# Squares of the weights behind the fourth hh eviction, and urgent evictions of hh, hl and ysb, in a two-layer mixture-of-experts kernel

## The chip, the cores and the metric

The kernel runs on one core of a Trainium2 chip. The metric is the device time of one execution in microseconds (us), the median of the runs given. One further execution was recorded by the hardware profiler; all rows and times by line below are from it. TensorE is PE in the rows (PEld its weight loads), VectorE is DVE, ScalarE is ACT, GpSimd is POOL, SyncE is SP; a "q" behind an engine's name is its instruction queue.

## The reference

Linear attention with a norm makes `x` of 4608 rows of 512; a first layer of experts sends each row to two of eight experts, a second sends rows with a positive score to one of eight. An expert is two matrices, 512 x 1024 and 1024 x 512, with a ReLU between:

```python
for e in range(E):                                   # first layer, k = 0, 1
    h = np.maximum(x[mask] @ w1[e], 0.0)
    out[mask] += top2_w[mask, k, None] * (h @ w2[e])
...
for e in range(E):                                   # second layer
    h = np.maximum(xc[mask] @ w1[e], 0.0)
    y[mask] = gate_w[mask, None] * (h @ w2[e])
```

## The kernel before

The stages follow each other: attention and routing up to about 240 us, the first layer of experts up to about 1130 us, then the second layer. All is computed in 16-bit pairs (high and low half), so each weight matrix is scaled and split before use.

The first layer runs through 38 groups, n = 0 to 37, of two tiles of 128 rows (three of them of one tile; the last group of an expert may have fewer rows than 256). For each group TensorE does layer 1 in four pieces of 24 matmuls (L227; a one-tile group has two pieces of 48), each into one of the three buffers of the PSUM pool pA. After each piece ScalarE writes `hh`, the ReLU's high half (L235), and VectorE `hl`, the low half (L236), which frees the buffer. Layer 2 (L263) takes for each tile g 16 matmuls with `hh`, in the order of the pieces, and 8 with `hl`; ScalarE scales its result into `ysb` (L1089), SP writes `ysb` to `ydram`, VectorE adds the other expert's row to make `x` (L1093), and GpSimd scatters it. Between the two tiles of layer 2 stand small matmuls that gate the group before (L952, from `x2T`, a DMA transpose of `xh`, which ScalarE and VectorE split out of `x` after a sum of squares `jk`), and behind them matmuls that rank its rows (L995, from `rm`, which VectorE makes of the gate's result).

Beside this runs the preparation of weights. The table `MATS` gives each group at most one matrix: F, a half of the next expert's weights of the first layer, or P, a half of the second layer's (`presplit`, written to DRAM by SP as `wsd`). A matrix takes these steps: a load of 2 MB into `stage` (two buffers) by SP; four squares with a running sum, `wjunk` (L169), on ScalarE; their sum `wsum` (L172) on VectorE; a small matmul over the partitions (L175) on TensorE; the scale `wscl`; four splits, each a copy on ScalarE (L185) and a difference on VectorE (L186), after which the `stage` buffer is free. The load and the squares are written in the matrix's own group (squares at points 4 to 7, after layer 2's first tile), the matmul and the splits in the group after it, at points 0 to 4.

TensorE's order is the order in which the code is written, in all groups. For the other engines it is so only up to group 2 and from group 35 on; between, a scheduler orders each engine's queue by priority, which is the order of the code, and by its own idea of when an instruction's inputs are there. Each queue is then run in that order on the chip: an instruction at the head that waits for a semaphore holds back what stands behind it.

Of the kernel before, what the change touches and what calls it, by code (L numbers as in the profile page):

```python
# [12 lines left out]
AF = mybir.ActivationFunctionType  # L13
# [5 lines left out]
N, D, E, F = 4608, 512, 8, 1024  # L19
# [28 lines left out]
ROUTE = (9, 12, 14, 14, 16, 22, 22, 22, 22, 22, 22, 28, 29, 32, 37, 40, 41, 43, 45, 46, 47, 50, 57, 57, 57, 61, 61)  # L48

LATER = 3  # L50
QTE = "AAVAAVAVVVAVAVVAVAVVVAVAAVAVVVAAAAAAAAAAAAAAVVAAAAAAAAAA"
OSBE = "VVVVAVAAAAAVVAAVAAVAVAAAAAVAAAAAAAAAAAAAAVAAAAAAAAAVAAAA"
SQE = "GGGAAAAAAAAGAAGAAAAAAAAAAAAAAAAAAAAAAAAAAAAAAAAAAAAAAAAA"
# [29 lines left out]
def moe_kernel(ctx: ExitStack, tc: tile.TileContext, q, k, v, g_norm, w_gate, w_noise, noise,  # L83
               w1, w2, w2_skip, w2_gate, w21, w22, out, dbg=None):
    nc = tc.nc
    V, A, G, PE, SP = nc.vector, nc.scalar, nc.gpsimd, nc.tensor, nc.sync
# [3 lines left out]
    wpools = [ctx.enter_context(tc.tile_pool(name="wpool0", bufs=1))]  # L90
    turn = {}
    stg = [None]

    def wtile(shape, dt, name, pool=None):

# [64 lines left out]
    def split_matrix(load, hi, lo, scale, kk, sc, inv):  # L160

        st = stg[0].tile([P, 4096], F32, name="stage")
        load(st)
        acc = tiny.tile([P, 4], F32, name="wacc")
        junk = tiny.tile([P, F], BF16, name="wjunk", bufs=1)
        kw = {} if scale is None else {"scale": scale}
        yield
        for c in range(4):
            A.activation(junk, st[:, F * c:F * c + F], AF.Square, accum_out=acc[:, c:c + 1], **kw)  # L169
            if c == 3:  # L170
                sums = tiny.tile([P, 1], F32, name="wsum")
                V.tensor_reduce(sums, acc, axis=AX.X, op=ALU.add)  # L172
            yield
        ps = pSm[0].tile([P, 1], F32, name="small")
        PE.matmul(ps, ones32, sums, start=True, stop=True)  # L175
        a0, i0 = pow2_scale(ps, kk, "wsc")
        if scale is None:
            V.tensor_copy(sc, a0)  # L178
        else:
            V.tensor_mul(sc, a0, scale)  # L180
        V.tensor_copy(inv, i0)
        for c in range(4):
            yield
            d = slice(F * c, F * c + F)
            A.activation(hi[:, d], st[:, d], AF.Copy, scale=sc)  # L185
            V.scalar_tensor_tensor(lo[:, d], st[:, d], sc, hi[:, d], op0=ALU.mult, op1=ALU.subtract)  # L186
# [44 lines left out]
    def layer1_out(ps, nt, hh, hl, fp):  # L231

        nf = 4 if nt <= P else 2
        fsl = slice(fp * nf, fp * nf + nf)
        A.activation(hh[:, fsl, 0:nt], ps, AF.Relu)  # L235
        V.scalar_tensor_tensor(hl[:, fsl, 0:nt], ps, 0.0, hh[:, fsl, 0:nt], op0=ALU.max, op1=ALU.subtract)  # L236

    def layer1_piece(W, xT, nt, hh, hl, fp):
        layer1_out(layer1_matmuls(W, xT, nt, fp), nt, hh, hl, fp)

    def layer1(W, xT, nt, point=None):
        hh = p2.tile([P, 8, 2 * P], F16, name="hh")
# [40 lines left out]
    with ExitStack() as st:  # L283
# [505 lines left out]
        for b in range(B):  # L789
# [3 lines left out]
            g = gate_columns(b)  # L793
# [252 lines left out]
    def moe1_group(n, W, xg, xT, step, point):  # L1046
        e, i0, ng, nt = groups[n]
        t0 = e * T1 + i0
        aux = xg[:, 0:ng, 512:528]
        gate = tiny.tile([P, 2], F32, name="gate")  # L1050
        if e:
            junk = tiny.tile([P, 8], F32, name="gjunk", bufs=1)
            for g in range(ng):
                V.scalar_tensor_tensor(junk, aux[:, g, 0:8], W[4], at_pos[:, e], op0=ALU.mult, op1=ALU.mult,
                                       accum_out=gate[:, g:g + 1])
        else:
            V.tensor_scalar(gate, aux[:, :, 0], W[4], None, op0=ALU.mult)
        h = layer1(W, xT, nt, point)
        if e:
            val = tiny.tile([P, ng], F32, name="val")  # L1060
            for g in range(ng):
                V.scalar_tensor_tensor(junk, pair_sum[:, e], aux[:, g, 8:9], before, op0=ALU.is_equal, op1=ALU.mult,
                                       accum_out=val[:, g:g + 1])
            fl = tiny.tile([P, ng], F32, name="fl")
            V.tensor_scalar(fl, val, float(TOP - BASE[e]), None, op0=ALU.is_gt)
            nf = tiny.tile([P, ng], F32, name="nf")
            V.tensor_scalar(nf, fl, -BIG, BIG, op0=ALU.mult, op1=ALU.add)
            row = tiny.tile([P, ng], F32, name="orow")
            V.tensor_sub(row, aux[:, :, 9], val)
            V.tensor_sub(row, row, own[:, i0:i0 + ng])  # L1070
            gi = tiny.tile([P, ng], I32, name="gi")
            V.tensor_add(gi, row, nf)
            oi = tiny.tile([P, ng], I32, name="oi")
            V.scalar_tensor_tensor(oi, idxp[:, t0:t0 + ng], -1.0, nf, op0=ALU.add, op1=ALU.add)
            yos = []
            for g in range(ng):
                yo = yob[turn_y[0] % 4]
                turn_y[0] += 1
                G.indirect_dma_start(out=yo, out_offset=None, in_=ydram[0:BASE[e], :],  # L1079
                                     in_offset=bass.IndirectOffsetOnAxis(ap=gi[:, g:g + 1], axis=0),  # L1080
                                     bounds_check=BASE[e] - 1, oob_is_err=False)
                yos.append(yo)
        step(0)
        x2 = p1.tile([P, 2, D], F32, name="x2", bufs=2)[:, 0:ng]
        for g in range(2):
            if g < ng:
                ps = layer2(W, h, g)
                ysb = p2.tile([P, D], F32, name="ysb", bufs=3)
                A.activation(ysb, ps, AF.Copy, scale=gate[:, g:g + 1])  # L1089
                if e < E - 1:  # L1090
                    SP.dma_start(ydram[BASE[e] + (i0 + g) * P:BASE[e] + (i0 + g + 1) * P, :], ysb)
                if e:
                    V.tensor_add(x2[:, g], ysb, yos[g])  # L1093
                    if n >= CUT + 2:
                        G.memset(spacer, 0.0)
                    s = G.indirect_dma_start(out=out, out_offset=bass.IndirectOffsetOnAxis(ap=oi[:, g:g + 1], axis=0),  # L1096
                                             in_=x2[:, g], in_offset=None, bounds_check=N - 1, oob_is_err=False)
                    nodep(s.ins, osc + rd2, "rows of other tokens")
                    osc.append(s.ins)
            step(1 + g)  # L1100
            point(4 + 2 * g)
            point(5 + 2 * g)
        return finalize(e, i0, ng, x2, fl) if e else None
# [188 lines left out]
    for n, (e, i0, _, _) in enumerate(groups):  # L1292
        if n == BEGIN:
            begin.close()
        if n + 1 < len(groups) and n <= BEGIN:
            xs[n + 1] = gather1(*groups[n + 1])
        if n + 2 < len(groups) and n >= BEGIN:
            xs[n + 2] = gather1(*groups[n + 2])
        if n == CUT + 2:
            order.enter_context(tc.manual_schedule(engines=engines))  # L1300
        old, cur = cur, matrix(mats[n])
        if cur:
            next(cur)

        def point(p, old=old, cur=cur):
            if old and p <= 4:
                next(old, None)
                if p == 4:
                    next(old, None)
            if cur and p >= 4:  # L1310
                next(cur)

        def step(k, prev=fin, last=last):
            g = last if k == 0 else prev
            if g is not None:
                next(g, None)
            if k == 0 and n == CUT + 2:
                pick_early()
            for i in range(2):
                for what in AHEAD[i].get((n, k), ""):  # L1320
                    if what == "g":
                        Ra.append(Rows(ahead[i]))
                        for _ in range(2):
                            Ra[i].gather(osc[early_out:])
                    elif what == "s":
                        Ra[i].split()
                    else:
                        dyn_weights(ewi[:, i:i + 1], 2 * i, Wa[i], "ab".index(what))

        step(-1)  # L1330
        if n == CUT + 2:
            splits.close()
            wpools.append(only1.enter_context(tc.tile_pool(name="wpool2", bufs=1)))
            p3 = only1.enter_context(tc.tile_pool(name="p3", bufs=2))
            p4 = xrow_pool.enter_context(tc.tile_pool(name="p4", bufs=1))
            for i in range(4):
                xo.append(p4.tile([P, 1, D], F32, name=f"x2r{i}"))
                G.memset(xo[i], 0.0)
        last = fin
        fin = moe1_group(n, Ws[e], *xs.pop(n), step, point)  # L1340

    next(fin)
# [16 lines left out]
    nr, nt = len(RTILES), 4 + sum(RTILES)  # L1359
# [157 lines left out]
    with flag(0):  # L1517
# [5 lines left out]
        st, cur = 1, 0  # L1523
        while st < nf:
            V.tensor_add(inc[:, 1 - cur, st:nf], inc[:, cur, st:nf], inc[:, cur, 0:nf - st])
            V.tensor_copy(inc[:, 1 - cur, 0:st], inc[:, cur, 0:st])
            cur, st = 1 - cur, st * 2
# [48 lines left out]
        with flag(NX // 2):  # L1576
# [18 lines left out]
            for e in range(E):  # L1595
                W = []
# [22 lines left out]
            for e in range(E):  # L1619
                W = []  # L1620
# [41 lines left out]
```

## Time and profile before

| | |
|---|---|
| time, three runs | 1353.91 us median (1352.23 to 1360.18) |
| profiled execution, its own time | 1369.16 us |
| its span | 1367.1 us |
| mean granted clock of TensorE | 0.957 |
| TensorE, VectorE, ScalarE, GpSimd busy | 1211.8, 818.6, 658.5, 379.0 us |
| moved by DMA | 293.34 MB, 215 GB/s |

The time is the span and about 2 us around it. A clock of 1 is 2.4 GHz; TensorE is granted either that or half of it. Busy time of TensorE is the union of its matmuls; the idle time between them is what the list of waits distributes over those who ended it.

### The profile page before, as it was taken

Reading aid. Unit: us, or ns where it says so; the run is one execution under the profiler, and the core shown is the slowest. Engines: PE = TensorE matmul, PEld = TensorE weight load, DVE = VectorE, ACT = ScalarE, POOL = GpSimd, SP = SyncE. Lnnn points to the kernel's source line nnn. Section 1 sums busy time; section 2 is a strip of 40 time slices with the busy share of each in tenths; the row PEclk is TensorE's granted clock in tenths of the full one; section 3 lists DMA queues with packets and bytes.
Section 4 is the critical chain, followed back from the end, with each engine's and each line's share of the span. In section 5 each row is a group of like instructions: output and inputs, shape, how many; then the busy total and the mean of one; then the engine's idle time right before and its main releaser. Section 6 shows DMA issues by size and latency. Waiting matters only on the chain.

```text
span 1367.1 us, 25295 instructions
## 1 busy us (share of the span) xinstructions
PE 1211.8 (89%) x9341; PEld 855.2 (63%) x9341; DVE 818.6 (60%) x3034; ACT 658.5 (48%) x1209; POOL 379.0 (28%) x454
## 2 busy tenths in 40 slices
PE   6777789997999989998999888798899989999995
PEld 6677677665666656656666655555566657566664
DVE  1667877344776685767568756655777755433321
ACT  1669562355755564656365556444566232222210
POOL 3322342113223223332322232223212322232220
PEclk9978799999999999999999999999999999999998
DMA  9989964867886885976778796869897475586680
GB/s 240 293 240 299 293 163 110 219 197 231 210 268 142 252 220 178 248 235 208 181 245 246 235 289 196 247 111 295 242 253 196 146 197 170 185 236 185 197 270 16
DMA packets 311410, 293.34 MB, mean 215 GB/s; under 512 B 205022, under 2 KB 256222, under 8 KB 307180
## 3 DMA queue, kind: packets, MB, share of 16 engines
q1 hardware_dynamic: 288316, 208.22, 57.5%
q0 software_dynamic: 22384, 82.36, 17.7%
q8 instruction: 75, 1.23, 0.4%
q10 hardware_dynamic: 576, 1.05, 0.2%
q14 instruction: 59, 0.48, 0.1%
HBM read 172.86 MB, written 93.42 MB: 195 GB/s over the span
## 4 chain that ended last, share of the span: by engine, by line
PE 33%; DVE 17%; issue 16%; DMA 16%; ACT 12%; POOL 4%; SPq 1%; POOLq 0%; ACTq 0%; DVEq 0%
PE b L263 16%; DMA stage<-in_moe_w_dram 13%; PE a L227 12%; ACT wjunk L169 4%; DVE wb L186 2%; DVE wa L186 2%; DVE hl L236 2%; ACT presplit L185 1%; PE b L473 1%; PE kvps L408 1%; ACT ysb L1089 1%; ACT hh L235 1%; POOL out_dram L1175 1%; DVE xh L925 1%; DVE rsc L971 1%
## 5 line engine op out<-in xcount | busy, mean ns | idle before, releaser
L227 PEld LDWEIGHTS <-wa 128*128 128x128 f16 x5184 | 465.6, 100 | 79.3 <-issue 14.6
L227 PE MATMUL a<-xT,wa 128*128 128x256 f16 (+6 forms) x3648 | 399.3, 271 | 25.3 <-DVE hl L236 21.8
L263 PE MATMUL b<-wb,hh 128*128 128x512 f16 x1488 | 348.5, 384 | 40.2 <-ACT hh L235 40.0
L263 PEld LDWEIGHTS <-hh 128*128 128x128 f16 x1488 | 140.2, 98 | 208.9 <-ACT hh L235 57.3
L235 ACT ACTIVATE hh<-a 128x512 f16<-128x512 f32 (+5 forms) x186 | 106.7, 577 | 208.4 <-PE a L227 195.2
L236 DVE SCALAR_TENSOR_TENSOR hl<-a,hh 128x512 f16<-128x512 f32 (+5 forms) x186 | 124.7, 674 | 101.5 <-ACT hh L235 90.9
L263 PE MATMUL b<-wb,hl 128*128 128x512 f16 x744 | 178.5, 383 | 0.0
L1096 POOL DMA_INDIRECT out_dram<-x,oi x67 | 69.2, 1032 | 281.0 <-DVE nact L1008 94.6
L1041 POOL DMA_INDIRECT xg<-xrows,idxp x67 | 68.2, 1018 | 274.1 <-DMA xT<-xg 108.5
L263 PEld LDWEIGHTS <-hl 128*128 128x128 f16 x744 | 73.8, 99 | 91.3 <-issue 5.8
L169 ACT ACTIVATE wjunk<-stage 128x1024 bf16<-128x1024 f32 x96 | 101.0, 1052 | 56.7 <-DMA stage<-in_moe_w_dram 50.6
L1089 ACT ACTIVATE ysb<-b,gate 128x512 f32<-128x512 f32 x73 | 49.8, 682 | 155.1 <-PE b L263 129.6
L227 PE MATMUL a<-x2Tr,wa 128*128 128x256 f16 (+1 forms) x1152 | 107.4, 255 | 1.5 <-DMA x2Tr<-xh 1.5
L1079 POOL DMA_INDIRECT yo<-ydram,gi x67 | 74.2, 1107 | 59.9 <-issue 22.7
L186 DVE SCALAR_TENSOR_TENSOR presplit<-stage,wscl,presplit 128x1024 f16<-128x1024 f32 x64 | 80.1, 1280 | 10.6 <-ACT presplit L185 10.1
L185 ACT ACTIVATE presplit<-stage,wscl 128x1024 f16<-128x1024 f32 x64 | 70.5, 1138 | 12.5 <-DVE wscl L178 12.5
L473 PE MATMUL b<-kvbd,qTs 128*128 128x160 f32 x256 | 53.3, 349 | 21.8 <-issue 10.0
L1093 DVE TENSOR_TENSOR x<-ysb,yo 128x512 f32<-128x512 f32 x67 | 46.1, 687 | 40.8 <-ACT ysb L1089 40.7
L921 ACT ACTIVATE jk<-x 128x512 bf16<-128x512 f32 x67 | 42.0, 627 | 50.3 <-DVE x L1093 49.5
L517 POOL TENSOR_TENSOR osb<-osb,rinv 128x1024 f32<-128x1024 f32 (+1 forms) x20 | 37.1, 1854 | 87.0 <-DVE rinv L145 71.4
L473 PEld LDWEIGHTS b<-kvbd,qTs 128*128 128x128 f32 x256 | 43.0, 220 | 26.5 <-issue 10.8
L924 ACT ACTIVATE xh<-x,x2ss 128x512 f16<-128x512 f32 x67 | 44.8, 714 | 26.9 <-DVE x2ss L136 22.8
(356 smaller groups left out, 1566.6 us busy)
## 6 DMA issues: line engine op xcount, KB each, us to landing
stage<-in_moe_w_dram SPq DMA_DIRECT2D x32, 2048.0 KB
wsd<-presplit SPq DMA_DIRECT2D x8, 2056.0 KB
ydram<-ysb SPq DMA_DIRECT2D x64, 256.0 KB
wsd<-presplit SPq DMA_DIRECT2D x8, 2048.0 KB
out_dram<-zeros SPq DMA_DIRECT2D x9, 1024.0 KB
km<-in_k_dram SPq DMA_DIRECT2D x16, 512.0 KB
vm<-in_v_dram SPq DMA_DIRECT2D x16, 512.0 KB
qm<-in_q_dram SPq DMA_DIRECT2D x16, 512.0 KB
```

The costliest lines, as they stand in the source:

```text
L169: A.activation(junk, st[:, F * c:F * c + F], AF.Square, accum_out=acc[:, c:c + 1], **kw)
L185: A.activation(hi[:, d], st[:, d], AF.Copy, scale=sc)
L186: V.scalar_tensor_tensor(lo[:, d], st[:, d], sc, hi[:, d], op0=ALU.mult, op1=ALU.subtract)
L227: PE.matmul(ps[:, i, :], a[:, c, fs], xT[:, b + c, 0:nt], start=(n == 0), stop=(n == 11))
L235: A.activation(hh[:, fsl, 0:nt], ps, AF.Relu)
L236: V.scalar_tensor_tensor(hl[:, fsl, 0:nt], ps, 0.0, hh[:, fsl, 0:nt], op0=ALU.max, op1=ALU.subtract)
L263: PE.matmul(ps, a[:, f, gsl], b[:, f, :], start=(fs.start == 0 and i == 0), stop=(fs.stop == 8 and a is hl and f == 7))
L473: PE.matmul(po[:, i, :], qT[:, i, :], kvb[b % 4][:, h0 + i, :], start=True, stop=True)
L1041: G.indirect_dma_start(out=xg[:, g], out_offset=None, in_=xrows, in_offset=bass.IndirectOffsetOnAxis(ap=idx[:, t0 + g:t0 + g + 1], axis=0))
L1079: G.indirect_dma_start(out=yo, out_offset=None, in_=ydram[0:BASE[e], :], in_offset=bass.IndirectOffsetOnAxis(ap=gi[:, g:g + 1], axis=0), b ...
L1089: A.activation(ysb, ps, AF.Copy, scale=gate[:, g:g + 1])
L1096: s = G.indirect_dma_start(out=out, out_offset=bass.IndirectOffsetOnAxis(ap=oi[:, g:g + 1], axis=0), in_=x2[:, g], in_offset=None, bounds_ ...
```

## The change

Two things, both in the order of the queues. First, from group 3 to group 35 each square of the weights gets an ordering edge, without a semaphore, behind the `hh` that was written last before it in the code; the squares are written after layer 1 of their group, so that is its fourth `hh`. Second, the priority of `hh`, `hl` and of the first layer's `ysb` is raised by 500, so that the scheduler puts them ahead of other instructions of the same engine that it finds ready at the same time. No computation, transfer or buffer is changed.

```diff
+URGENT = 500
...
+    behind = [None, False]
...
         for c in range(4):
-            A.activation(junk, st[:, F * c:F * c + F], AF.Square, accum_out=acc[:, c:c + 1], **kw)
+            with tc.issue_after(behind[0]) if behind[1] else ExitStack():
+                A.activation(junk, st[:, F * c:F * c + F], AF.Square, accum_out=acc[:, c:c + 1], **kw)
...
-        A.activation(hh[:, fsl, 0:nt], ps, AF.Relu)
+        behind[0] = A.activation(hh[:, fsl, 0:nt], ps, AF.Relu).ins
...
-        layer1_out(layer1_matmuls(W, xT, nt, fp), nt, hh, hl, fp)
+        ps = layer1_matmuls(W, xT, nt, fp)
+        with tc.high_priority(offset=URGENT):
+            layer1_out(ps, nt, hh, hl, fp)
...
-                A.activation(ysb, ps, AF.Copy, scale=gate[:, g:g + 1])
+                with tc.high_priority(offset=URGENT):
+                    A.activation(ysb, ps, AF.Copy, scale=gate[:, g:g + 1])
...
         if n == BEGIN:
             begin.close()
+            behind[1] = True
...
         if n == CUT + 2:
             splits.close()
+            behind[1] = False
```

TensorE's queue is the same in both kernels, instruction for instruction. On SP and GpSimd a handful of neighbours change places; in both kernels the load into `stage` stands on SP behind the group's first `ydram` write where the group splits a P half, and ahead of it elsewhere. The changes are on ScalarE and VectorE.

ScalarE at the end of group 16 and the start of group 17, before (line numbers are those of each kernel; x2 means two in a row; the `hh` with 192 columns is the first of group 17):

```order
L185 ACTIVATE wb<-stage,wscl 128x1024
L169 ACTIVATE wjunk,wacc<-stage 128x1024
L235 ACTIVATE hh<-a 128x512
L169 ACTIVATE wjunk,wacc<-stage 128x1024 x3
L1089 ACTIVATE ysb<-b,gate 128x512
L921 ACTIVATE jk,ss_8015<-x_7862 128x512
L973 ACTIVATE rdf<-rdf 128x16
L169 ACTIVATE wjunk,wacc<-stage,gcol 128x1024 x2
L1089 ACTIVATE ysb<-b,gate 128x512
L169 ACTIVATE wjunk,wacc<-stage,gcol 128x1024
L921 ACTIVATE jk,ss_8015<-x_7862 128x512
L235 ACTIVATE hh<-a 128x2x192
```

The same place on ScalarE in the changed kernel, from the fourth split of group 16 to the first `ysb` of group 17:

```order
L188 ACTIVATE wb<-stage,wscl 128x1024
L238 ACTIVATE hh<-a 128x512
L1095 ACTIVATE ysb<-b,gate 128x512
L926 ACTIVATE jk,ss_8015<-x_7862 128x512
L978 ACTIVATE rdf<-rdf 128x16
L1095 ACTIVATE ysb<-b,gate 128x512
L926 ACTIVATE jk,ss_8015<-x_7862 128x512
L238 ACTIVATE hh<-a 128x2x192
L929 ACTIVATE xh<-x_7862,x2ss 128x512 x2
L238 ACTIVATE hh<-a 128x2x192 x3
L172 ACTIVATE wjunk,wacc<-stage 128x1024 x4
L1095 ACTIVATE ysb<-b,gate 128x512
```

The squares of two matrices that stood around the fourth `hh` of group 16, its two `ysb` and the first `hh` of group 17 are gone from there; those of the first of the two are now one block behind group 17's fourth `hh`, and those of the second (with `gcol`) one group later, in the same place.

VectorE in group 17, before:

```order
L236 SCALAR_TENSOR_TENSOR hl<-a,hh 128x2x192
L971 TENSOR_SCALAR rsc_8233<-x2ss,rsk 128x2
L172 TENSOR_REDUCE wsum<-wacc 128x1
L925 SCALAR_TENSOR_TENSOR xh<-x_7862,x2ss,xh 128x512 x2
L236 SCALAR_TENSOR_TENSOR hl<-a,hh 128x2x192 x3
L957 TENSOR_REDUCE rL<-small 128x18
L960 SCALAR_TENSOR_TENSOR act<-rL,fl 128x2
```

VectorE there in the changed kernel:

```order
L976 TENSOR_SCALAR rsc_8233<-x2ss,rsk 128x2
L930 SCALAR_TENSOR_TENSOR xh<-x_7862,x2ss,xh 128x512 x2
L239 SCALAR_TENSOR_TENSOR hl<-a,hh 128x2x192 x3
L175 TENSOR_REDUCE wsum<-wacc 128x1
L962 TENSOR_REDUCE rL<-small 128x18
L965 SCALAR_TENSOR_TENSOR act<-rL,fl 128x2
```

`wsum` has moved with its squares, from ahead of `xh` to behind the last `hl`; behind it stand `rL` and the rest of the gate's small operations, with `x` among them, and `rm`.

## Rows read from the trace of the kernel before

**Rows 1.** The page's first part: busy us (share of the span) xinstructions, by engine

```profile
PE 1211.8 (89%) x9341; PEld 855.2 (63%) x9341; DVE 818.6 (60%) x3034; ACT 658.5 (48%) x1209; POOL 379.0 (28%) x454
```

**Rows 2.** TensorE's waits, 336.8 to 1066.4 us: us in total, times, longest

```profile
PE b L263 <- ACT hh L235: 32.7, 27, 4.3
PE a L227 <- DVE hl L236: 21.8, 9, 4.2
PE small L995 <- DVE rm L988: 5.9, 2, 3.2
PE small L952 <- DMA x2T<-xh: 3.4, 2, 2.3
```

**Rows 3.** Stretches: us, busy by engine (PE first), clock, DMA share, GB/s

```profile
336.80:1066.40 729.60, 664.37 (x5101) 447.46 (x5100) 494.39 (x2010) 412.14 (x707) 207.38 (x211) 0.97 0.81 226
427.30:448.90 21.60, 21.60 (x172) 14.84 (x171) 16.17 (x68) 10.57 (x17) 11.35 (x11) 1.00 0.83 199
...
635.30:661.50 26.20, 21.97 (x170) 15.14 (x169) 11.83 (x58) 10.40 (x21) 4.95 (x5) 0.87 0.59 140
...
804.30:832.30 28.00, 23.80 (x172) 15.00 (x171) 15.95 (x68) 14.94 (x25) 9.95 (x9) 0.94 0.91 262
```

**Rows 4.** Timeline of ScalarE at 638 us: start, duration, instruction, [idle before, releaser]

```profile
638.67 1.15 ACT L169 ACTIVATE wjunk<-stage,gcol 128x1024 bf16<-128x1024 f32 x1 [5.19 <-DMA stage<-in_moe_w_dram]
...
643.41 0.47 ACT L235 ACTIVATE hh<-a 128x384 f16<-128x384 f32 x1
```

**Rows 5.** Timeline of TensorE beside it, layer 1 of group 17

```profile
635.31 6.10 PE L227 MATMUL a<-xT,wa 128*128 128x192 f16 x72
645.64 4.00 PE L227 MATMUL a<-xT,wa 128*128 128x192 f16 x24 [4.23 <-DVE hl L236]
```

**Rows 6.** Timeline of all engines in group 9 (448.9 to 471.3 us)

```profile
461.41 1.05 ACT L169 ACTIVATE wjunk<-stage 128x1024 bf16<-128x1024 f32 x1
...
462.45 0.59 ACT L235 ACTIVATE hh<-a 128x512 f16<-128x512 f32 x1
...
463.09 1.04 PE L263 MATMUL b<-wb,hh 128*128 128x512 f16 x4 [0.69 <-ACT hh L235]
...
463.56 0.40 SPq L200 DMA_DIRECT2D stage<-in_moe_w_dram  x1
...
466.34 0.67 ACT L1089 ACTIVATE ysb<-b,gate 128x512 f32<-128x512 f32 x1
...
468.95 0.17 DVE L988 TENSOR_TENSOR rm<-roh,act 128x16 f16<-128x16 f32 x1
...
471.27 0.17 PE L995 MATMUL small<-rm,tri 128*128 128x16 f16 x1
```

**Rows 7.** The squares (L169), 336.8 to 1066.4 us: duration min/median/max, and waits before them

```profile
L169 ACT ACTIVATE wjunk<-stage x84: 1040/1052/1057, 348.0 to 1037.5; 128x1024 bf16<-128x1024 f32 x84
L169 ACT ACTIVATION_READ_ACCUMULATOR wjunk<-stage x84: 185/188/199, 348.9 to 1038.5; 128x1 f32 x84
L169 ACT ACTIVATE wjunk<-stage,gcol x20: 1134/1147/1149, 406.8 to 892.4; 128x1024 bf16<-128x1024 f32 x20
...
  DMA stage<-in_moe_w_dram: 69.8, 16
```

**Rows 8.** Timeline of all engines in group 8, as layer 2 begins

```profile
438.06 3.62 PE L263 MATMUL b<-wb,hh 128*128 128x512 f16 x16
...
439.09 0.59 ACT L235 ACTIVATE hh<-a 128x512 f16<-128x512 f32 x1
```

**Rows 9.** The chain that ended last, 790 to 960 us: start, us, what

```profile
797.81 0.32 SPq L1091
...
798.18 17.34 DMA stage<-in_moe_w_dram
...
920.93 18.29 DMA stage<-in_moe_w_dram
```

**Rows 10.** The stretch after the stall of group 17; columns as in rows 3

```profile
644.80:651.60 6.80, 5.96 (x31) 4.49 (x31) 3.88 (x13) 2.79 (x7) 0.00 (x0) 0.50 0.51 98
```

## The prediction

> **What bounds the kernel now.** I read the shares by engine first: TensorE is busy 89% of the span, VectorE 60%, ScalarE 48% [rows 1]. So the question is what TensorE waits for, and only in the part that the change touches: groups 4 to 34 of the first layer of experts, 336.8 to 1066.4 us. The reader is to see three things there.
>
> First, the list of TensorE's waits in that part [rows 2]: 27 waits of layer 2 for `hh` (32.7 us) and 9 of layer 1 for `hl` (21.8), together 54.5 us. Two waits for `rm` (5.9) and two for `x2T` (3.4) are another matter.
>
> Second, the table by stretch [rows 3]: in the group that begins at 427.3 (one of three that look alike) TensorE is busy for all of its 21.6 us at full clock; the group at 635 us, with fewer rows, takes 26.2 at a mean clock of 0.87, the one at 804 us 28.0 at 0.94. So an undisturbed group of 256 rows takes 21.6 us, and the rest is loss.
>
> Third, who makes `hh` late. In ScalarE's timeline at 638 us the queue's head is a square of the weights, which has waited 5.19 us for its `stage` load; behind it stand `ysb`, two more squares, `jk`, and only then, at 643.41, the first `hh` of the next group [rows 4]. TensorE had done three pieces of layer 1 by 641.4, found no free PSUM buffer (pA has three) and stood 4.23 us [rows 5]. That is the long form. The short form is one square of 1.05 us between the last split and the fourth `hh`: the square starts at 461.41, `hh` at 462.45, and layer 2, which needs it after its first 12 matmuls, loses 0.69 us [rows 6]. I followed ScalarE's queue at each of the 36 waits: in 35 a square stands ahead of the late `hh`, waiting or running, in this piece or earlier in the group. The exception is 1.5 us in the one-tile group at 985 us, where `hh` stands behind `xh`. ScalarE's own list says the same from the other side: for 69.8 us, 16 times, it sat with a square at its head that waited for `stage` [rows 7].
>
> **The change part by part.** *Squares behind the fourth `hh`.* Nothing is added or removed: the 104 squares of 1.05 to 1.15 us in these groups [rows 7] go to one place, after the fourth `hh` of their own group and ahead of its first `ysb`, so that no `hh` stands behind a square in its own group, and none of the next group behind one that still waits for a load issued late in this one. This removes, of the 54.5 us, all but what stays: 1.5 for the `hh` behind `xh`; an estimated 1 in the one-tile groups, whose second `hh` stays behind a split; and 3 for `hh` that follow late splits. The last is from [rows 6]: without the square the fourth `hh` would start at 461.41 and end at 462.0, about 0.4 us ahead of its need, so the cover is bare; where the splits come later still, some of the wait stays, and I take 0.3 us in each of ten such groups.
>
> What the new place costs: four squares with their accumulator reads (1.05 and 0.19 us, [rows 7]) take 4.9 us. The fourth `hh` of the undisturbed group ends at 439.68, 12.4 us after the group's start and 1.6 after layer 2's [rows 8], so the squares end at 17.3, while layer 2's first half, 5.2 us long, has ended at 16.0. The first `ysb` is 1.3 us late and ends at 18.0. Queued behind it are `jk`, `rdf`, the second `ysb` and the next group's `hh` on ScalarE, the `ydram` write on SP, the scatter on GpSimd, and `x` on VectorE, which stands ahead of `rm`, for which TensorE waits at the group's end. In the trace `rm` ends at 469.12, 2.1 us after `ysb` at 467.01, and TensorE uses it at 471.27 without a wait [rows 6]; so here `rm` comes at 20.1 against a need just ahead of 21.6. The cover is some 1.4 us, and the new place costs nothing as long as the stage has landed by 1.4 us after the fourth `hh`. Past that each us of lateness is one us of TensorE. A load starts when a split has freed its buffer, at 463.56 for instance, 14.7 us into its group [rows 3, 6]; loads of the chain of waits take 10 to 12 us mostly, but 17.34 and 18.29 at 798 and 921 us [rows 9]. With 11 they land 4 us into the next group, far ahead; with 18, and a start at 18 behind `ysb`, at 14 to 15. I charge three such places with 2 us each, 6 us.
>
> *Evictions marked urgent.* No instruction more; on VectorE `wsum` now stands behind the four `hl` and ahead of `rL`, `hl` here and there ahead of one half of `xh`, and the second `x` a few small operations earlier. What moves later by one eviction (0.6 us) is `x2T`, for which TensorE waited twice, 3.4 us in all [rows 2]. I take nothing either way; at most those two waits and a few like them grow by 0.6 each.
>
> *The clock.* A mean of 0.97 over 729.6 us [rows 3] is 22 us at most, if TensorE had had work in all of it. In the stretch after the stall of 4.23 us, 6.8 us at 0.50 (1.2 GHz), it was busy 5.96 us [rows 10], so 3.0 of 3.4 were lost; at that ratio it is 19 us in all. Two such stretches follow the `rm` waits, which stay; I take 16 us back. The Trainium skill, "TensorE: Matmul & The Clock Gate", section Terms, prices throttled time at that time multiplied by one minus the ratio of the clocks, whether the engine has work or not; by that the term would be 3 us larger.
>
> *Sum.* 54.5 less 1.5, 1, 3 and 6 is 43; with the clock 59 us. The profiled execution took 1369.2 us, so 1310; it is 15.3 us above the median of the three runs. If all of that were waits for loads that profiling lengthened, the gain unprofiled would be 44; if none, 59. Most of the 43 lies in the queue's order and not in the length of a load, so I take 56: 1353.9 less 56 is 1298 us.
>
> **The rivals.** *DMA takes over.* The same bytes must move in 59 us less. The 16 DMA engines are at 0.81 in the section, and at 0.91 in the busiest group shown, with 262 GB/s [rows 3]; in 670 us the share would be 0.88. If they hold no more than 0.85 in the mean (the undisturbed group stands at 0.83), the section takes 729.6 x 0.81 / 0.85 = 695 us: a gain of 34, 1320 us. For it: loads of 17 and 18 us, where writes of `wsd` run beside them. Against it: a group at 0.83 ran without one wait. The Trainium skill, "DMA: Bandwidth & Descriptors", section Specifications, gives ceilings of 358 and 435 GB/s, by which 246 GB/s would be far from any bound and this rival would fall. The trace disagrees: 0.91 at 262 GB/s puts a full load of these transfers at 288 GB/s. So I keep it.
>
> *Slower: a ring through SP.* Where a group splits a `presplit` half, the next load stands behind the first `ydram` write on SP: at 798.18 it began 0.37 us after that write, which had waited for `ysb` [rows 9]. With squares in front of every such `ysb` this closes a ring: load, 4.9 us of squares, 0.7 of `ysb`, 0.4 of SP, next load. With 11 us it is 17, under a group's 21.6; it decides from loads of 15.6 us on, and the kernel is slower than before from 17.8 in all of the 26 groups with squares (2.2 us each against the 56). At 19 us it costs 88 and gives 1298 + 88 = 1386 us. Against it: about half of the groups have the load ahead of the write, and most loads take 10 to 12 us.
>
> *The order changes and the waits stay*, since `hh` then waits for splits that are themselves late: only the long form shortens, by some 10 us, 1344 us. Against it: the undisturbed group has the same four splits between its `hh` [rows 8].
>
> **How the numbers follow.** The forecast 0.75, DMA 0.13, waits stay 0.07, the ring 0.05. The forecast's own range is 1277 (all 54.5 and 22 gone) to 1310 (44 back); to leave out no more than 2 in 10 I go up to 1322, over the DMA case. One per cent, about what a measurement of this kernel can tell from no change, is 1340 to 1367: faster 0.88, same 0.07, slower 0.05.
>
> **What would show it.** In the changed kernel's section TensorE's waits for `hh` and `hl` fall from 54.5 to under 12 us; ScalarE's wait for `stage` from 69.8 to under 15; groups of 256 rows stand at 21.6 to 22.5 us; the mean clock is 0.99; the DMA share rises to 0.87 to 0.90. The step on the cover is wrong if TensorE's wait for `rm` grows well past 5.9, with a square before `ysb` that is seen to wait; the DMA rival has come if `x2T` or `xT` are TensorE's longest waits. It would be wrong as a whole if the 36 waits had a second cause of equal length right behind the squares.

## The result, and the profile after

The changed kernel takes 1296.01 us in the median of four runs (1292.01 to 1302.45), the kernel before beside it 1357.05 (1352.23 to 1361.32). The ratio is 0.9556, with a 95% interval of 0.9495 to 0.9616. The forecast was 1298. The profiled execution took 1299.42 us (span 1297.3); that of before took 1369.16.

Busy time and share of the span by engine, from the page of the changed kernel; TensorE is busy 21.6 us less than in [rows 1] and for a larger share:

```profile
PE 1190.2 (92%) x9341; PEld 848.2 (65%) x9341; DVE 814.9 (63%) x3034; ACT 665.8 (51%) x1209; POOL 374.4 (29%) x454
```

Groups 4 to 34 now run from 337.86 to 998.75 us: 660.9 us for the 729.6 of before. TensorE's waits there, all that are over 1 us in total; they answer to [rows 2], where `hh` and `hl` stood at 54.5:

```profile
PE small L1000 <- DVE rm L993: 5.1, 2, 2.7
PE small L957 <- DMA x2T<-xh: 4.2, 3, 2.3
PE b L268 <- ACT hh L238: 3.8, 6, 0.9
```

The waits for `hl` are gone, six for `hh` are left, and `rm` and `x2T` make 9.3 us together, as before. That they agree to a tenth is chance: in a second profile of the same kernel (the control below) they make 13.7. The stretches, columns as in [rows 3]: the section, group 9, and group 24 (the one at 804 us in [rows 3]):

```profile
337.86:998.75 660.89, 647.49 (x5100) 443.25 (x5099) 490.66 (x2010) 419.03 (x707) 202.57 (x211) 0.99 0.88 249
445.04:466.63 21.59, 21.59 (x171) 14.85 (x170) 16.67 (x68) 14.95 (x25) 6.81 (x7) 1.00 0.98 281
...
763.08:786.27 23.19, 21.94 (x171) 14.62 (x170) 16.78 (x68) 14.83 (x25) 7.07 (x8) 1.00 1.03 295
```

The reader is to see two things. TensorE did the same matmuls, some 5100, in 17 us less of busy time, and group 9 fills its 21.59 us with them although the DMA engines stand at 0.98. Of the 31 groups 18 now last 21.5 to 21.7 us; before it were five.

The squares themselves: ScalarE's list of waits has no `stage` any more (69.8 us, 16 times, in [rows 7]). The load is issued from two lines of the code; for each, the time from issue to landing:

```profile
DMA to landing us min/median/max: 9.6/11.7/14.2
...
DMA to landing us min/median/max: 9.4/12.4/15.4
```

And group 9 in the timeline of all engines, the same group as [rows 6]:

```profile
455.79 3.62 PE L268 MATMUL b<-wb,hh 128*128 128x512 f16 x16
...
457.31 0.59 ACT L238 ACTIVATE hh<-a 128x512 f16<-128x512 f32 x1
...
457.79 1.05 ACT L172 ACTIVATE wjunk<-stage 128x1024 bf16<-128x1024 f32 x1
...
462.39 0.67 ACT L1095 ACTIVATE ysb<-b,gate 128x512 f32<-128x512 f32 x1
...
464.68 0.17 DVE L993 TENSOR_TENSOR rm<-roh,act 128x16 f16<-128x16 f32 x1
...
466.55 0.17 PE L1000 MATMUL small<-rm,tri 128*128 128x16 f16 x1
```

Layer 2 runs through its 16 matmuls without a stop, the first square starts as the fourth `hh` ends (the two records overlap by 0.11 us), and `ysb` starts 17.4 us after the group's start, as the read of the fourth square's sum ends. It ends at 18.0 and `rm` at 19.8, 1.7 us ahead of its use; the forecast had put these at 18.0 and 20.1.

### The profile page after: what moved, and what is told of

Read it like the earlier page. It is cut to its first block, busy times and chain, and to the rows that moved or that the text cites. A ratio compares the mean times of both kernels' runs of the same rounds, so it can differ in the third digit from the quotient of the medians.

```text
span 1297.3 us, 25298 instructions
## 1 busy us (share of the span) xinstructions
PE 1190.2 (92%) x9341; PEld 848.2 (65%) x9341; DVE 814.9 (63%) x3034; ACT 665.8 (51%) x1209; POOL 374.4 (29%) x454
## 3 DMA queue, kind: packets, MB, share of 16 engines
q10 hardware_dynamic: 576, 1.05, 0.3%
## 4 chain that ended last, share of the span: by engine, by line
PE 56%; issue 12%; DVE 12%; DMA 7%; ACT 7%; POOL 3%; SPq 2%; POOLq 0%; DVEq 0%; ACTq 0%
PE b L268 26%; PE a L230 25%; DMA x2T<-xh 3%; PE b L478 1%; PE kvps L413 1%; DVE x L529 1%; DVE xh L930 1%; ACT wjunk L172 1%; DMA x2Tr<-xh 1%; POOL out_dram L1181 1%; DVE ohp L659 1%; ACT wb L188 1%; DMA yo<-ydram,gi 1%; DVE x L1099 1%; ACT x L526 1%
## 5 line engine op out<-in xcount | busy, mean ns | idle before, releaser
L230 PE MATMUL a<-xT,wa 128*128 128x256 f16 (+6 forms) x3648 | 392.5, 269 | 0.9 <-DMA xT<-xg 0.9
L268 PE MATMUL b<-wb,hh 128*128 128x512 f16 x1488 | 339.7, 380 | 10.9 <-ACT hh L238 10.7
L268 PEld LDWEIGHTS <-hh 128*128 128x128 f16 x1488 | 141.2, 98 | 171.6 <-ACT hh L238 17.3
L1102 POOL DMA_INDIRECT out_dram<-x,oi x67 | 68.7, 1026 | 213.0 <-DVE nact L1013 102.8
L478 PE MATMUL b<-kvbd,qTs 128*128 128x160 f32 x256 | 54.7, 356 | 22.6 <-issue 10.9
L175 DVE TENSOR_REDUCE wsum<-wacc 128x1 f32<-128x4 f32 x32 | 5.0, 156 | 92.9 <-ACT wjunk L172 92.9
L522 POOL TENSOR_TENSOR osb<-osb,rinv 128x1024 f32<-128x1024 f32 (+1 forms) x20 | 37.1, 1854 | 87.0 <-DVE rinv L147 65.2
```

The lines of the kernel that those rows point to most:

```text
L230: PE.matmul(ps[:, i, :], a[:, c, fs], xT[:, b + c, 0:nt], start=(n == 0), stop=(n == 11))
L268: PE.matmul(ps, a[:, f, gsl], b[:, f, :], start=(fs.start == 0 and i == 0), stop=(fs.stop == 8 and a is hl and f == 7))
L478: PE.matmul(po[:, i, :], qT[:, i, :], kvb[b % 4][:, h0 + i, :], start=True, stop=True)
```

## The experiments

All ratios are to the kernel before on the same chip. "Section" is groups 4 to 34 of the profiled execution; the unedited changed kernel had 660.9 us there in its first profile and 664.8 in a second (the control below), so a few us of a section are no finding. The kernel before took 1357 to 1366 us on the chips used, so medians from different chips are compared by their ratios.

| kernel | median us | ratio, 95% interval | section us | `hh` and `hl` waits there |
|---|---|---|---|---|
| before | | 1 | 729.6 | 54.5 |
| changed | 1296.01 | 0.9556 (0.9495 to 0.9616) | 660.9 | 3.8 |
| a1 edge only | 1302.59 | 0.9533 (0.9481 to 0.9585) | 666.8 | 2.4 |
| a2 urgent only | 1355.95 | 0.9943 (0.9910 to 0.9977) | 719.3 | 47.7 |
| b1 before, no squares | 1290.33 | 0.9456 (0.9388 to 0.9524) | 667.4 | 4.7 |
| b2 changed, no squares | 1292.87 | 0.9474 (0.9404 to 0.9545) | 665.8 | 7.3 |
| a3 one more square | 1294.16 | 0.9456 (0.9396 to 0.9517) | 667.1 | 6.6 |
| a4 three more squares | 1317.84 | 0.9640 (0.9589 to 0.9692) | 690.5 | 30.0 |
| c4 the same, scale first | 1298.31 | 0.9524 (0.9473 to 0.9575) | 664.8 | 10.3 |
| b3 more bytes | 1312.76 | 0.9600 (0.9539 to 0.9660) | 671.2 | 3.3 |
| b4 wsum and rank | 1292.18 | 0.9476 (0.9412 to 0.9539) | 666.1 | 3.4 |
| c1 control | 1300.96 | 0.9529 (0.9489 to 0.9570) | 664.8 | 4.5 |
| c2 late rank | 1287.91 | 0.9433 (0.9396 to 0.9470) | 649.0 | 3.7 |
| c3 early squares | 1281.37 | 0.9398 (0.9359 to 0.9437) | 656.7 | 7.8 |

### Which of the two parts

The edge alone:

```diff
-        with tc.high_priority(offset=URGENT):
-            layer1_out(ps, nt, hh, hl, fp)
+        layer1_out(ps, nt, hh, hl, fp)
...
-                with tc.high_priority(offset=URGENT):
-                    A.activation(ysb, ps, AF.Copy, scale=gate[:, g:g + 1])
+                A.activation(ysb, ps, AF.Copy, scale=gate[:, g:g + 1])
```

> The changed kernel with the priorities of hh, hl and ysb left as they were before, and the squares still behind the fourth hh. Theory of the forecast (the place of the squares in ScalarE's queue is the whole cause): about 1296 us, 1290 to 1302, TensorE's waits for hh and hl under 8 us in groups 4 to 34. Rival (the urgent evictions do a good part of the work): 1310 us or more.

And the urgency alone:

```diff
-            behind[1] = True
+            behind[1] = False
```

> The changed kernel without the ordering edge; only hh, hl and ysb are marked urgent. In its order a square still stands ahead of the fourth hh in most groups with a matrix, and squares still stand between ysb and the next hh. Theory of the forecast: 1340 to 1360 us, hh and hl waits of 45 us or more. Rival (urgency would be enough): 1296 to 1315 us.

The edge alone gives 0.9533 (its median, 1302.59, is that of a chip on which the kernel before took 1362.77), the control of the whole change 0.9529. The urgency alone gives 0.9943. TensorE's waits in the section with the urgency alone:

```profile
PE b L268 <- ACT hh L238: 27.8, 25, 3.7
PE a L230 <- DVE hl L239: 19.9, 9, 4.3
```

ScalarE's timeline there, in the place of [rows 4]; the first row is the square that waits at the queue's head, the second the first `hh` of the next group:

```profile
637.05 1.15 ACT L172 ACTIVATE wjunk<-stage,gcol 128x1024 bf16<-128x1024 f32 x1 [5.31 <-DMA stage<-in_moe_w_dram]
...
641.17 0.47 ACT L238 ACTIVATE hh<-a 128x384 f16<-128x384 f32 x1
```

The square at the queue's head waits for its load as before, and `hh` stands behind it: the raised priority did not move `hh` ahead of it. That the scheduler took the square to be ready earlier than it was is the likely reason; the trace shows the order, and not what the scheduler assumed. The edge is the change; the urgency adds at most the half per cent that it gives alone, and beside the edge nothing that these intervals show.

### Nothing but the squares

Both kernels with all squares left out; their sums are set to one, so the scale is another number:

```diff
-            A.activation(junk, st[:, F * c:F * c + F], AF.Square, accum_out=acc[:, c:c + 1], **kw)
+            if c == 0:
+                G.memset(acc, 1.0)
```

> The kernel before with all squares of the stage left out (their sums are set to one, so the scale is another): nothing stands ahead of hh but splits. Theory of the forecast (all but a few of the 54.5 us of hh and hl waits are squares, running or waiting for their load): 1285 to 1300 us, hh and hl waits under 8 us. Rival (a second cause of equal length right behind the squares): 1325 us or more, with the same waits named after another releaser's cause.

> The changed kernel with the same squares left out. If the new place is fully covered, the squares cost nothing and it takes 1288 to 1298 us. If the cover is thin, as charged in the forecast (6 us, and some 2 us in each place with a late load): 1282 to 1290 us. If the squares still hold up ysb and rm in each group: 1275 us or less.

TensorE's waits in the section of the kernel before without squares, of which only the second row is `hh`:

```profile
PE small L996 <- DVE roh L968: 5.7, 2, 3.3
PE b L264 <- ACT hh L236: 4.5, 8, 1.2
```

The kernel before loses its 54.5 us but for 4.7 by this one removal, so there is no second cause of that size behind the squares. And without squares both kernels stand at the section of the changed one (667.4 and 665.8 beside 660.9 and 664.8): at the new place the 104 squares of the section and their sums, 116 us of ScalarE's busy time (419.0 us with them, 302.7 without), cost nothing that can be measured. By their ratios the two kernels lie 7 to 10 us below the control, with intervals that overlap its own; 6 to 8 us of that is what groups 0 to 3 gained (87.3 and 86.8 us; 95.1 in the changed kernel, 93.4 in the control), where the squares stand in the order of the code in both kernels.

### How much the new place can bear

More squares behind the four and ahead of the first `ysb`, their results not used. So that the edge from `ysb` can point at them, the squares are written ahead of layer 2, and with them what else stood at point 4, the fourth split of the matrix before. This holds in groups 0 to 2 as well; there the squares then run ahead of `ysb`, which is a change of its own. `MORE` is 1 or 3.

```diff
+            if c == 3 and behind[1]:
+                with tc.issue_after(behind[0]):
+                    for i in range(MORE):
+                        ahead_of[0] = A.activation(junk, st[:, F * i:F * i + F], AF.Square, **kw).ins
...
         step(0)
+        ahead_of[0] = None
+        for p in range(4, 8):
+            point(p)
...
-                with tc.high_priority(offset=URGENT):
+                with tc.high_priority(offset=URGENT), tc.issue_after(ahead_of[0]) if ahead_of[0] else ExitStack():
                     A.activation(ysb, ps, AF.Copy, scale=gate[:, g:g + 1])
...
-            point(4 + 2 * g)
-            point(5 + 2 * g)
```

> The changed kernel with one square more (1.05 us, its result is not used) behind the four, ahead of the first ysb, for each of the 27 matrices from group 3 on. Forecast's step on the cover (about 1.4 us between rm and its need): it is hidden, 1292 to 1304 us. Rival (no cover is left at the new place): 25 x 1.05, so 1320 us or more, with rm as the wait.

> The same with three squares more (3.2 us, not used) ahead of the first ysb. With a cover of 1.4 us some 1.8 us show in each of 25 groups: 45 us, 1341 us, as TensorE's wait for rm of about 1.8 us in each. Rival, a larger cover of 2.5 us or more: under 1315 us. Rival, no cover: 1370 us or more.

One more square is free within what two profiles of one kernel differ by: 667.1 us in the section. The medians do not show it by themselves, since in both kernels groups 0 to 3 are 11 to 13 us shorter by the change of their own (82.5 us with one more square). Three more squares cost 26 to 30 us in the section, less than the 45 expected, and through another wait: `rm` stands at 6.1, inside the range of the unedited kernel (5.1 and 9.4).

```profile
PE b L274 <- ACT hh L244: 26.9, 38, 1.4
PE small L1006 <- DVE rm L999: 6.1, 2, 3.3
```

The timeline of this kernel, from `ysb` of group 9 to the stalls of group 10, shows the way:

```profile
464.21 0.17 DVE L999 TENSOR_TENSOR rm<-roh,act 128x16 f16<-128x16 f32 x1
...
465.83 0.67 ACT L1104 ACTIVATE ysb<-b,gate 128x512 f32<-128x512 f32 x1
...
466.53 0.69 DVE L1108 TENSOR_TENSOR x<-ysb,yo 128x512 f32<-128x512 f32 x1 [0.59 <-DMA xg<-xrows,idxp]
...
468.59 0.69 DVE L1108 TENSOR_TENSOR x<-ysb,yo 128x512 f32<-128x512 f32 x1 [0.79 <-ACT ysb L1104]
...
473.61 0.17 DVE L1001 COPY vals<-idv 128x4 f16<-128x4 f16 x1 [1.74 <-POOL rhs L1033]
...
474.36 1.40 DVE L936 SCALAR_TENSOR_TENSOR xh<-x,x2ss,xh 128x512 f16<-128x512 f32 x2
475.68 0.15 DVE L187 COPY wscl<-wscs 128x1 f32<-128x1 f32 x1
475.86 1.15 ACT L194 ACTIVATE presplit<-stage,wscl 128x1024 f16<-128x1024 f32 x1 [3.00 <-DVE wscl L187]
...
480.11 1.04 PE L274 MATMUL b<-wb,hh 128*128 128x512 f16 x4 [0.95 <-ACT hh L244]
480.99 0.59 ACT L244 ACTIVATE hh<-a 128x512 f16<-128x512 f32 x1
```

The two `x` are those of the group's two tiles. A late `ysb` makes them late, behind `x` on VectorE stand `vals`, the two halves of `xh` and then the scale `wscl`; the splits of the next group wait for `wscl`, the fourth `hh` stands behind the splits, and the next squares behind it. That closes a ring. GpSimd is on it too: `vals` waits 1.74 us for its `rhs`, and such waits make 26.4 us in the section (15 times), 4.2 in the changed kernel.

The first row shows why `rm` did not move. Here, as in most groups of this kernel, the scheduler set `rm` ahead of `x` on VectorE, and a late `ysb` can't reach it there; in the changed kernel `x` stands ahead of `rm` in the same group (18.0 and 19.6 us after its start). So this run does not test the way through `rm` that the forecast had followed. With one more square `x` still stands ahead of `rm` in most groups; in the same group `x` then starts 1.2 us later and `rm` 0.6, and the waits for `rm` do not grow (4.8 us). The groups on the ring last 23.5 us instead of 21.6: the three squares, 1.09 us each, bring 3.3 and show 1.9, so in this order of the queues the ring had 1.4 us of room. To test that it is this ring, the small operations of the scale are marked urgent, which puts `wscl` ahead of `xh`:

```diff
-        a0, i0 = pow2_scale(ps, kk, "wsc")
...
+        with tc.high_priority(offset=URGENT):
+            a0, i0 = pow2_scale(ps, kk, "wsc")
...
```

> The kernel with three more squares, and in it the small operations of the scale wscl marked urgent too, so that on VectorE they stand ahead of the two halves of xh (1.5 us). Theory formed on its trace (the added squares act through a ring: squares, ysb, x, xh on VectorE, wscl behind it, splits, fourth hh, squares; 23.5 us long in that run): the ring falls to 22 us or less, the hh waits from 26.9 to under 10 us, the time by 20 us or more, to 1300 us or less. Rival (the added squares hold up hh in another way, or the wait moves to rm): 1310 us or more.

TensorE's waits in the section:

```profile
PE b L275 <- ACT hh L245: 8.6, 11, 1.8
PE small L1007 <- DVE rm L1000: 4.5, 2, 2.5
```

and the same place in group 10, where `wscl` is done before `xh` and layer 2 has no stall:

```profile
466.30 0.14 DVE L188 COPY wscl<-wscs 128x1 f32<-128x1 f32 x1
466.42 1.41 DVE L937 SCALAR_TENSOR_TENSOR xh<-x,x2ss,xh 128x512 f16<-128x512 f32 x2
466.48 2.19 ACT L195 ACTIVATE presplit<-stage,wscl 128x1024 f16<-128x1024 f32 x2 [1.05 <-DVE wscl L188]
...
471.36 3.62 PE L275 MATMUL b<-wb,hh 128*128 128x512 f16 x16
```

The section is back at 664.8 with the three squares still in it; by the ratios (0.9640 and 0.9524) the time fell by some 16 us, less than the 20 expected. The waits of `vals` for GpSimd stay (24.4 us, 15 times), so they do not make the ring too long by themselves. The scheduler also put the last two `hh` of a group next to each other, behind the third split instead of around it; how much of the 26 us this did was not taken apart.

### Room on the DMA engines

A copy of 0.5 MB from DRAM to DRAM behind each load, not used:

```diff
-        load(st)
+        loaded = load(st)
+        if behind[1]:
+            with tc.issue_after(loaded.ins):
+                SP.dma_start(twice[len(spares) % 4], xrows[P * len(spares):P * len(spares) + 2 * P, 0:512])
+            spares.append(0)
```

> The changed kernel with a copy of 0.5 MB from DRAM to DRAM, not used, behind each load of a matrix, on the same queue: 13 MB on top of 165 in groups 4 to 34, 8%, so the DMA share would go from 0.88 to 0.95. Theory of the forecast (room is left, loads land ahead of the squares): at most 1304 us, loads land about 2 us later. Rival (DMA is at its bound now): the groups lengthen with the bytes, by 3% or more of 661 us, 1316 us or more, with x2T, xT or stage as the waits.

The section as a stretch, columns as before:

```profile
343.57:1014.73 671.16, 650.83 (x5101) 442.54 (x5099) 490.34 (x2010) 417.87 (x707) 206.07 (x212) 0.99 0.94 266
```

8% more bytes lengthened the section by 6 to 10 us, 1 to 1.6%. The engines stood at 0.94 in the mean. The median, 1312.76, lies between the two expectations; by the ratio, 0.9600, the cost is 0.5 to 0.7% beside the changed kernel and its control, inside the intervals. ScalarE does not wait for `stage` here either. But TensorE's longest wait is now `x2T`, which is one of the waits that the rival named:

```profile
PE small L963 <- DMA x2T<-xh: 6.5, 4, 2.1
```

That is 2 us more than in the changed kernel (4.2) and its control (4.3); 4.6 us of waits without a named cause (last section) stand beside it. There is room, and not much of it.

### A version that is faster than both

What was left in the profile after: in group 3 `wsum` stood on VectorE behind a gate product that waited for a gather, and TensorE lost 7.4 us; in the one-tile groups 26, 31 and 36 the rank follows the gate at once, so TensorE waits for `rm`. The kernel b4 changes both:

```diff
+            with tc.issue_after(summed[0]) if BEGIN <= n <= BEGIN + 2 else ExitStack():
...
+            if later and p == 0:
+                next(later.pop())
...
-            if g is not None:
+            if k == 2 and g is not None and groups[n][2] == 1:
+                later.append(g)
+            elif g is not None:
                 next(g, None)
```

> The changed kernel with two more moves. In groups 3 to 5 the first gate products stand behind the wsum that is written before them (in the trace wsum stood behind one that waited 5.3 us for a gather, and TensorE lost 7.4 us in group 3). And in the three one-tile groups the rank of the group before goes behind the first piece of layer 1 of the next group instead of right behind the gate (waits for rm of 2.7, 2.5 and 4.6 us). Theory: 7 + 9.7 us less, and some 5 us of half clock behind them, so 1274 us, 1270 to 1284. Rival (other waits take their place: x2T, or the splits of group 3): 1288 us or more.

1292.18 us, 0.9476: a miss, above the 1288 us of the rival, and by the intervals not told apart from the changed kernel. Groups 0 to 3 took 85.5 us (95.1) and groups 35 to 37 60.9 (65.9), but group 5 took 32.6 instead of 21.6 by a stall that had no cause in the program (last section), and group 23 lost 3.8 to a `yo` gather that landed late. So the late rank was run again by itself, beside the unedited kernel:

> The changed kernel once more, unedited, beside the others of this batch: 0.949 to 0.962 of the kernel before, as in its own runs; groups 4 to 34 at 661 to 667 us.

> The changed kernel with only the rank moved in the three one-tile groups, behind the first piece of layer 1 of the next group. By the batch before (groups 26 to 28 shorter by 8 us, 31 and 32 by 3, 36 and 37 by 5): 12 to 16 us less than the control. Rival (what that batch gained came from group 3 alone): within 4 us of the control.

The control came out as expected (0.9529, 664.8 us). The late rank alone (the second and third piece of the diff) takes 1287.91 us beside the control's 1300.96, 13 us less, and the intervals do not overlap. TensorE's waits in its section have no `rm` any more:

```profile
PE b L269 <- ACT hh L239: 3.7, 6, 0.9
PE small L958 <- DMA x2T<-xh: 1.9, 2, 1.6
PE small L179 <- DVE fl L1071: 1.0, 1, 1.0
```

Last, both moves and in groups 0 to 2 the squares written ahead of layer 2:

```diff
         step(0)
+        if n < BEGIN:
+            for p in range(4, 8):
+                point(p)
...
```

> The rank moved, the first gate products behind wsum in groups 3 to 5, and in groups 0 to 2, which keep the order of the code, the squares written ahead of layer 2 instead of after its tiles. Groups 0 to 3 took 82.5 us with that in the run with one more square, 95.1 in the changed kernel. Theory: 12 us there and 12 from the rank, 1265 to 1278 us beside 1296, 0.935 of the kernel before. Rival (groups 4 and 5 give it back, as in that run, 5.7 us, or with the stall without a named cause seen in group 5, 10 us): 8 to 16 us less than the control.

| us by stretch | groups 0 to 3 | 4 to 34 | 35 to 37 |
|---|---|---|---|
| c1 control | 93.4 | 664.8 | 65.3 |
| c2 late rank | 97.2 | 649.0 | 62.3 |
| c3 early squares | 82.5 | 656.7 | 62.4 |

c3 takes 1281.37 us, 0.9398 (0.9359 to 0.9437) of the kernel before and 19.6 us less than the control: the fastest of all that ran, and 3 us above its expectation. Groups 0 to 3 give 10.9 of the 12 expected; in 4 to 34 group 5 takes 25.5 us instead of the 21.6 of the changed kernel's first profile, in waits for `hl` and `hh`, which is the part of the rival that came, and about half of the 7.7 us by which its section is longer than that of c2. The intervals of c2 and c3 overlap, so how much the early squares add to the late rank is not settled.

## Why the prediction was right, step by step

**The cause** was read rightly. That a square stands ahead of the late `hh`, waiting or running, is seen at 35 of 36 waits; with the squares taken away the waits are gone (b1), with the edge alone too (a1), and with the urgency alone they stay (a2). The marks in the changed profile came as told: `hh` and `hl` under 12 us (3.8), `stage` on ScalarE under 15 (none), the clock at 0.99, the DMA share at 0.87 to 0.90 (0.88). That groups of 256 rows stand at 21.6 to 22.5 us holds for most; groups 21, 24, 27, 28 and 32 took 22.8 to 25.6.

**The sum**, 59 us in the profiled execution, was too small; the section shortened by 68.7. Its terms:

- *Idle time:* 43 forecast, 51.8 measured (65.2 us of TensorE's idle time in the section before, 13.4 after). The 6 us charged for late loads did not come: the slowest load took 15.4 us, where the chain of waits had shown 17.34 and 18.29 [rows 9]. Of the 5.5 us that were to stay, 3.8 stayed. This is the term that was mis-sized most, though by how much depends on the profile taken: the control's gives 46.7.
- *The clock:* 16 forecast, 12.5 measured (TensorE was busy 36.7 us at half clock in the section before and 11.8 after, and half of such time is lost); 14.4 by the control's profile. Three groups (27, 28 and 32) had a half-clock stretch behind waits for `rm` or `x2T`; the forecast had counted two.
- *A term that was not in the sum:* 4.4 us. Busy time fell by 16.9, from 664.37 [rows 3] to 647.49, and the clock explains 12.5. What the rest is was not tested. It fits what a stop adds to the busy time itself: after its stall in [rows 6] four matmuls took 1.04 us, where a quarter of the 16 in [rows 8] is 0.91, and 0.13 us for each of some 30 stops fewer is an estimated 3.9 us. The control's profile leaves 3.6.

**From profile to median:** the profiled executions differ by 69.7 us, the medians by 61.0. The forecast took 3 off for that; it would have needed 9. The profile of the kernel before had caught an execution slower than the four that were timed; how much of that lay in the waits that the change removes was a guess, and too low. The misses in the sum and in this step are of opposite sign: the gain of 56 us was measured as 61.0. And the kernel before, taken at 1353.9 from three runs, stands at 1357.05 with the fourth. So 1298 came nearer to 1296 than its terms deserve, by luck.

**The cover.** In group 9 `rm` came 1.7 us ahead of its use, where the forecast had 1.4. The start of `ysb` at 17.4 us, forecast at 17.3, is right by two errors that cancel: the fourth `hh` ended 0.5 us later than reckoned (12.9 for 12.4), and the squares took 4.6 us for 4.9, since the reads of their sums overlap with the squares. One more square fits, as the step said. What shows first beyond that was not foreseen: with three more the scheduler set `rm` ahead of `x`, so the step was not put to the test, and what became late was the next group's `hh`, through `xh`, `wscl` and the splits. The sentence that the second `ysb`, `jk` and the next group's `hh` stand behind the squares was there; that VectorE passes the delay on to the splits was not followed. That this way had 1.4 us of room as well is chance.

**Urgency** at nothing either way: `rm` and `x2T` at 9.3 us before and after (13.7 in the control), 12.4 without the urgency, and a ratio of 0.9533 without it.

**The rivals.** DMA took over nowhere: its premise was that the engines hold no more than 0.85 in the mean, and they hold 0.88 here, 0.98 in group 9 without a wait, and 0.94 with more bytes. Nor is 288 GB/s what a full load moves, as the prediction read from one group: in the trace of the kernel before itself, from 800 to 815 us, 397 GB/s were moved at a share of 1.05. The ring through SP did not close: it was to decide from loads of 15.6 us on, the slowest took 15.4, and ScalarE never waited for `stage`. A ring there is, but through VectorE; in the order that three more squares brought it decides from 1.4 us of added work on. That the waits stay because `hh` waits for late splits can be true of no more than the 3.8 us that are left.

## What to carry to other kernels

In a queue that runs in order, work that waits for a load belongs behind the last instruction that the busiest engine needs from that queue in this round; raising the priority of the needed instructions alone did not do it here (0.994, where the edge alone gave 0.953). Price the new place by following every queue that the moved block delays until it comes back to the block itself, since the wait that appears may be one that closes such a ring. A dose of added work helps to find it, but read the order of the queues again in the dosed kernel: here the scheduler had changed it at the very place that was to be tested. After a change of this kind look at the rounds that are shorter than the rest: here the one-tile groups and the first groups held another 20 us.

## What the runs showed of the hardware that was not expected

In b4 TensorE lost 6.1 us in group 5 to nothing that the profile names. Its waits from 349 to 365 us, and the weight loads in that stretch:

```profile
PE a L232 <- issue: 6.1, 9, 1.1
```

```profile
355.25 0.10 PEld L232 LDWEIGHTS <-wa 128*128 128x128 f16 x1 [0.61 <-issue]
355.96 0.10 PEld L232 LDWEIGHTS <-wa 128*128 128x128 f16 x1 [0.61 <-issue]
356.68 0.10 PEld L232 LDWEIGHTS <-wa 128*128 128x128 f16 x1 [0.62 <-issue]
357.39 0.10 PEld L232 LDWEIGHTS <-wa 128*128 128x128 f16 x1 [0.62 <-issue]
358.12 0.11 PEld L232 LDWEIGHTS <-wa 128*128 128x128 f16 x1 [0.63 <-issue]
```

One weight load every 0.71 to 0.73 us, evenly, for some 10 us, with no semaphore waited for; the half clock that was granted from 357.8 us on, for 10 us, cost 3.6 us more. The same sign stood in b3 (13 times, 4.6 us in the section), in b2 (6 times, 4.2 us in the whole run), in b1 (6 times, 2.6 us) and in the kernel before (twice, 1.5 us). The DMA share was 0.91 in the ten us ahead of it in b4 and 0.44 during it; no run here tested a cause, and it stays open.

The DMA share of a stretch can read 1.03 (group 24) and TensorE still wait for only 1.25 us in it. So a share near one does not show by itself that transfers bound the time.

Two executions of one kernel can differ by 4 us in one group: group 23 took 21.6 us in the first profile of the changed kernel and 26.0 in the control's, with a wait for `rm` of 4.2. There `x`, which stands ahead of `rm` on VectorE, waited 5.5 us for the `yo` gather; in b4 the same gather cost it 4.8.
